# Attention with a gated convolution network on one core: neighbouring PSUM bank pairs, and exponentials that depend on all maxima of their score set

## The chip, the core and the metric

The kernel runs on one core of a Trainium2 chip. The core has five engines, each with its own in-order queue of instructions: TensorE (PE in the profile, with its weight loads shown as PEld), VectorE (DVE), ScalarE (ACT), GpSimd (POOL) and SyncE (SP, which issues DMAs). They meet through semaphores: an instruction can wait until another engine's semaphore has reached a value. Matmuls write into PSUM, which has eight banks of 512 float32 columns on 128 partitions; DVE and ACT read it. The metric is the device time of one execution in microseconds.

## What is computed

Eight batches, eight heads, 576 positions, head dimension 64. Attention is block causal with blocks of 64, and its output goes through a gated network with a convolution of width 3 along the sequence:

```python
scores = (1 / np.sqrt(D)) * np.matmul(q, k.transpose(0, 1, 3, 2))
scores = np.where(block_i >= block_j, scores, -1000000000.0)
scores = scores - np.max(scores, axis=-1, keepdims=True)
attn = np.exp(scores)
attn = attn / (np.sum(attn, axis=-1, keepdims=True) + 1e-09)
out = np.matmul(attn, v)
...
h = np.maximum(x @ w_in, 0.0)                      # x: heads side by side, 512 wide; h: 1024 wide
conv_out = sum(conv_w[k] * hp[:, k:k + S, :] for k in range(3))
gate = 1.0 / (1.0 + np.exp(-conv_out))
return h * gate @ w_out
```

The network's products are split into high and low parts (three products each), so FFN work takes the larger share of the matmul instructions' columns.

## The kernel before

**The work.** A visit handles two heads of one batch. The first batch is cut into a part A (blocks 0 to 3 of the sequence) and a part B (blocks 4 to 8); from the second batch on, a visit takes all nine blocks, and there are 28 such visits. The score matmuls (line L1000) of a visit come in sets that each fill two PSUM banks, one per head: blocks 8 and 5, blocks 7 and 6, and blocks 4, 3, 2, 1, 0 (in part A one set of four blocks, in part B the last set is block 4 alone). For each block of a set, DVE takes the row maxima of both heads in one instruction (`mx`, L1012, it reads both banks), and ACT one exponential for each head (`ex`, L1017, it reads one bank, writes the tile p and sums its rows). In the program an exponential depends on the maximum of its own block. A few small instructions on the statistics tile st then merge the two 32-row halves (L1031, L686, L1038 to L1052), POOL scales the probabilities (L1064), DVE transposes them (L1083), and PE multiplies them with v (L1096) into two more banks. From these ACT writes the high part of x (L1110), and DVE the low part (L1113); DVE reads both banks.

**The network (FFN).** When the four visits of a batch have written x, `ffn` multiplies with w_in (L1143, one bank per 128 columns of the hidden layer), ACT takes the relu (L1157) and one convolution tap (L1160), DVE the other two taps (L1164, L1168), ACT the tanh (L1173), DVE the gate (L1176), ACT and POOL make its high and low part (L1180, L1183), and PE multiplies with w_out (L1209) into one bank; ACT copies the result out (L1217) and SP stores it. FFN matmuls of one batch are mixed with the attention of the next. Dummy matmuls (L1304) fill planned gaps of PE.

**What sets the order.** All of this is recorded as operations with durations, dependencies and buffers. `Plan.order` then runs a list scheduler over them: each operation has a number in the table TARGETS (in twentieths of a microsecond) by which a ready operation is preferred, and the scheduler also hands out the PSUM banks. Its function `vacant` says whether banks are free for an operation that needs one or two; the loop at the end of `order` picks them. In the kernel before, the two banks of a set can be any two free ones: `both` makes a view of them with a step, so the pair (1, 4) is read as `banks[:, 1:5:3]`. The order that comes out is written engine by engine into the program, and the framework below derives the semaphore waits from what each instruction reads and writes.

Of the kernel before, what the change touches and what calls it, by code (L numbers as in the profile page):

```python
# [18 lines left out]
PE, DVE, ACT, POOL, SP = 0, 1, 2, 3, 4  # L19

TARGETS = """
# [238 lines left out]
class Plan:  # L260
# [53 lines left out]
    def order(self, targets, skip, fill, clock, pair):  # L314
# [26 lines left out]
        n = len(slots)  # L341
# [11 lines left out]
        def vacant(o, t):  # L353
# [3 lines left out]
            ask = {}  # L357
            for b in need:
                ask[b.tag] = max(ask.get(b.tag, 0), b.index + 1)
            at = sorted(freed[z] for z in range(n) if tenant[z] is None)  # L360
            if len(at) < len(need):
                return None, need
            own = kept[0] if t < kept[2] else kept[1]
# [30 lines left out]
        while left:  # L394
# [49 lines left out]
            t, _, e, o, where = best  # L444
# [896 lines left out]
```

## Time and profile before

| | |
|---|---|
| time, median of 3 runs | 851.78 us (849.61 to 852.69) |
| the profiled execution | 848.9 us, of which the span from first to last instruction is 847.0 us |
| PE busy | 722.5 us (85%) |
| DVE busy | 598.7 us (71%) |
| ACT busy | 536.1 us (63%) |
| POOL busy | 446.4 us (53%) |
| mean granted TensorE clock | 0.959 of full speed |
| chain of work that ended last, by engine | PE 20%, DVE 17%, ACT 16%, POOL 9% |

Busy times are unions of instruction spans, so an engine's idle time is the span less its busy time: 124.5 us on PE. In the lists of waits a line names the instruction before which an engine sat idle, and what ended the idle time; waits under 0.15 us are not counted. The granted clock is 1 at 2.4 GHz and 0.5 at 1.2 GHz.

### The profile page before, as it was taken

Reading aid. Unit: us, or ns where it says so; the run is one execution under the profiler, and the core shown is the slowest. Engines: PE = TensorE matmul, PEld = TensorE weight load, DVE = VectorE, ACT = ScalarE, POOL = GpSimd, SP = SyncE. Lnnn points to the kernel's source line nnn. Section 1 sums busy time; section 2 is a strip of 40 time slices with the busy share of each in tenths; the row PEclk is TensorE's granted clock in tenths of the full one; section 3 lists DMA queues with packets and bytes.
Section 4 is the critical chain, followed back from the end, with each engine's and each line's share of the span. In section 5 each row is a group of like instructions: output and inputs, shape, how many; then the busy total and the mean of one; then the engine's idle time right before and its main releaser. Section 6 shows DMA issues by size and latency. Waiting matters only on the chain.

```text
span 847.0 us, 29994 instructions
## 1 busy us (share of the span) xinstructions
PE 722.5 (85%) x12111; PEld 578.5 (68%) x12111; DVE 598.7 (71%) x1422; ACT 536.1 (63%) x1987; POOL 446.4 (53%) x926
## 2 busy tenths in 40 slices
PE   8788877777788898789989899879798968898998
PEld 6557656554666777476868677767676857677887
DVE  4698998665686858658777858677677836857453
ACT  5565656755676748457677658675677646567454
POOL 2455676554456553538456754556355725644332
PEclk9999999998999999899999999899999978999999
DMA  7925543334332422333313251333324232121001
GB/s 187 195 47 123 108 107 72 57 65 78 70 58 55 80 49 55 63 65 72 70 37 75 49 119 30 83 58 84 58 48 94 41 72 43 29 56 30 27 26 38
DMA packets 238671, 58.59 MB, mean 69 GB/s; under 512 B 228652, under 2 KB 233028, under 8 KB 238532
## 3 DMA queue, kind: packets, MB, share of 16 engines
q1 hardware_dynamic: 237988, 56.55, 32.0%
q8 instruction: 95, 1.56, 0.8%
q14 instruction: 44, 0.36, 0.2%
q10 hardware_dynamic: 544, 0.13, 0.1%
HBM read 47.21 MB, written 9.44 MB: 67 GB/s over the span
## 4 chain that ended last, share of the span: by engine, by line
PE 20%; DVE 17%; ACT 16%; POOL 9%; issue 4%; DMA 0%; POOLq 0%; SPq 0%; DVEq 0%; ACTq 0%
ACT p L1017 9%; PE banks L1143 9%; DVE st L1012 6%; POOL p L1064 6%; PE banks L1209 5%; PE banks L1000 3%; PE banks L1096 3%; DVE ptw L1083 3%; POOL gl L1183 2%; DVE t L1164 2%; ACT t L1160 2%; DVE t L1168 1%; ACT h L1157 1%; ACT t L1173 1%; DVE t L1176 1%
## 5 line engine op out<-in xcount | busy, mean ns | idle before, releaser
L1017 ACT ACTIVATE p<-banks,st 128x160 f32<-128x160 f32 (+8 forms) x576 | 221.3, 395 | 153.4 <-DVE st L1012 130.1
L1064 POOL TENSOR_SCALAR p<-p,st 128x32 f32<-128x32 f32 (+8 forms) x576 | 246.1, 445 | 120.2 <-DVE st L1052 110.5
L1143 PE MATMUL banks<-x,wih 128*128 128x290 f32 (+3 forms) x1024 | 206.7, 315 | 33.1 <-DVE st L1012 15.5
L1143 PEld LDWEIGHTS banks<-x,wih 128*128 128x128 f32 x1024 | 164.9, 199 | 54.2 <-DVE st L1012 18.1
L1012 DVE TENSOR_REDUCE st<-banks 128x2 f32<-128x320 f32 (+8 forms) x288 | 132.3, 481 | 90.8 <-ACT p L1017 34.2
L1183 POOL TENSOR_TENSOR gl<-t,gh 128x289 fp32r<-128x289 f32 (+3 forms) x128 | 109.5, 866 | 115.1 <-ACT gh L1180 102.9
L1083 DVE STREAM_TRANSPOSE ptw<-p 128x576 f32<-128x576 f32 (+8 forms) x272 | 130.4, 502 | 31.5 <-POOL p L1064 30.8
L1209 PE MATMUL banks<-woh,gh 128*128 128x512 f32 (+1 forms) x296 | 122.7, 414 | 24.1 <-DVE st L1012 14.8
L1000 PE MATMUL banks<-kT,qT 64*32 64x128 f32 (+8 forms) x4320 | 107.8, 316 | 22.7 <-DVE st L1012 5.0
L1143 PE MATMUL banks<-x,wil 128*128 128x288 f32 (+3 forms) x512 | 114.9, 311 | 11.3 <-DVE st L1012 7.1
L1209 PE MATMUL banks<-woh,gl 128*128 128x512 f32 (+1 forms) x296 | 118.4, 400 | 5.0 <-POOL gl L1183 4.7
L1017 ACT ACTIVATION_READ_ACCUMULATOR p<-banks,st 128x1 f32 x576 | 118.0, 205 | 0.0
L1209 PE MATMUL banks<-wol,gh 128*128 128x512 f32 (+1 forms) x296 | 116.9, 395 | 0.0
L686 POOL TENSOR_SCALAR st<-st 32x16 f32<-32x16 f32 (+2 forms) x136 | 32.8, 241 | 142.1 <-ACT p L1017 94.9
L1000 PEld LDWEIGHTS banks<-kT,qT 64*32 64x32 f32 x4320 | 70.1, 110 | 53.9 <-issue 15.3
L1164 DVE SCALAR_TENSOR_TENSOR t<-h,cw,t 128x289 f32<-128x289 f32 (+3 forms) x128 | 72.4, 573 | 42.3 <-ACT t L1160 40.4
L1096 PE MATMUL banks<-ptw,vn 64*32 64x224 f32 (+8 forms) x4608 | 93.9, 300 | 9.3 <-issue 6.1
L1143 PEld LDWEIGHTS banks<-x,wil 128*128 128x128 f32 x512 | 87.0, 200 | 17.1 <-DVE st L1012 9.8
L1096 PEld LDWEIGHTS banks<-ptw,vn 64*32 64x32 f32 x4608 | 80.6, 106 | 26.3 <-issue 10.7
L1209 PEld LDWEIGHTS banks<-woh,gh 128*128 128x128 f32 x296 | 57.0, 193 | 46.9 <-DVE st L1012 20.6
L1173 ACT ACTIVATE t<-t 128x289 f32<-128x289 f32 (+3 forms) x128 | 57.0, 447 | 33.0 <-DVE t L1168 32.1
L1157 ACT ACTIVATE h<-banks 128x290 f32<-128x290 f32 (+3 forms) x128 | 50.8, 407 | 40.5 <-PE banks L1143 30.9
(91 smaller groups left out, 859.1 us busy)
## 6 DMA issues: line engine op xcount, KB each, us to landing
vn<-in_v_dram SPq DMA_DIRECT2D x128, 144.0 KB, 3.7
out_dram<-stage SPq DMA_DIRECT2D x35, 256.0 KB, 2.1
qn<-in_q_dram SPq DMA_DIRECT2D x112, 72.0 KB, 2.8
kn<-in_k_dram SPq DMA_DIRECT2D x112, 72.0 KB, 2.6
x<-in_moe_w_out_dram SPq DMA_DIRECT2D x8, 512.0 KB, 4.1
gl<-in_moe_w_in_dram SPq DMA_DIRECT2D x4, 512.0 KB, 5.7
gh<-in_moe_w_in_dram SPq DMA_DIRECT2D x3, 512.0 KB, 4.1
vxa<-in_v_dram SPq DMA_DIRECT2D x16, 64.0 KB, 3.4
```

The costliest lines, as they stand in the source:

```text
L1000: nc.tensor.matmul(both(sb)[32 * quad:32 * quad + 32, h, o:o + w].rearrange("p (u n) -> p u n", n=32), t["q"].ap[r, 64 * b + 32 * g:64 * b ...
L1012: nc.vector.tensor_reduce(out=st.ap[:, c:c + 2], in_=both(sb)[:, :, off:off + w], op=ALU.max, axis=AX.X, negate=True)
L1017: nc.scalar.activation(out=pt.ap[:, h, :], in_=both(sb)[:, h, off:off + w], func=AF.Exp, bias=st.ap[:, c:c + 1], accum_out=st.ap[:, n + c: ...
L1064: nc.gpsimd.tensor_scalar(out=pt.ap[:, h, :], in0=pt.ap[:, h, :], scalar1=st.ap[:, 5 * n + c:5 * n + c + 1], scalar2=0.0, op0=ALU.mult, op ...
L1083: nc.vector.transpose(pt.ap[:, :, b:b + rise * b + 1:rise, :], x.ap.rearrange("p h (u n) -> p h u n", n=32))
L1096: nc.tensor.matmul(both(vb)[o:o + 32, g, 32 * (lo - b0):32 * (b1 - b0)].rearrange("p (b n) -> p b n", n=32), vat(u, h)[r, 32 * y:32 * y + ...
L1143: nc.tensor.matmul(fb.ap[:, 0:n2], wt[:, c, fs], xs[c][xi].ap[:, x0:x0 + n2], start=(n + c - c0 == 0), stop=(n + c - c0 == 3 * NCC - 1))
L1157: nc.scalar.activation(out=hb.ap[:, 0:n2], in_=fb.ap[:, 0:n2], func=AF.Relu, scale=0.5)
L1164: nc.vector.scalar_tensor_tensor(out=t.ap[:, i0:no], in0=hb.ap[:, own + i0 - 1:own + no - 1], scalar=cw[:, f:f + 1], in1=t.ap[:, i0:no], o ...
L1173: nc.scalar.activation(out=t.ap[:, 0:no], in_=t.ap[:, 0:no], func=AF.Tanh)
L1183: nc.gpsimd.tensor_tensor(out=gbuf[1].ap[:, f, carry:carry + no], in0=t.ap[:, 0:no], in1=gbuf[0].ap[:, f, carry:carry + no], op=ALU.subtract)
L1209: nc.tensor.matmul(fb.ap[:, 0:cut], gbuf[a].ap[:, f, cs], w[:, f, ds], start=(f == 0 and n == 0), stop=(f == NFC - 1 and n == 2))
```

## The change

Four edits, and a new table of numbers.

1. An operation that needs two banks gets an even bank and its right neighbour (0 and 1, 2 and 3, 4 and 5, 6 and 7); one that needs a single bank prefers one whose neighbour is taken. `both` is then a plain contiguous slice. This concerns the score sets (L1000, L1012, L1017) and the banks from which x is read (L1096, L1110, L1113).
2. In a score set all maxima are recorded before the exponentials, and each exponential depends on all of them.
3. The planner's durations for four small copies of the statistics (L1031, L686) are 0.23 and 0.26 in place of 0.15 and 0.2. They change no instruction.
4. TARGETS is another table of the same length. The count of every kind of instruction stays as it was, but for one dummy matmul more (173 for 172). The lines after the edits move by 10 to 13: L1000 is L1010, L1012 is L1023, L1017 is L1028, L1096 is L1109, L1113 is L1126, L1143 is L1156, L1209 is L1222.

```diff
--1214 -1250 -926 -958 -1097 -783 -1374 -1285 -1001 -1007 -709 -742 -948 -909 -960 -790 -625 -807 -914 -36 -288 91 883 731 552 -182 -412 857 -202 120
...
-            at = sorted(freed[z] for z in range(n) if tenant[z] is None)
-            if len(at) < len(need):
+            if len(need) == 2:
+                at = [max(freed[z], freed[z + 1]) for z in range(0, n, 2) if tenant[z] is None and tenant[z + 1] is None]
+            else:
+                at = [freed[z] for z in range(n) if tenant[z] is None]
+            if not at:
                 return None, need
...
-            return at[len(need) - 1], need
+            return min(at), need
...
+            need = [b for b in o.banks if b.slot is None]
+            if len(need) == 2:
+                z = min((max(freed[z] + o.ldw, freed[z + 1] + o.ldw, o.start), last[z] != need[0].tag, z)
+                        for z in range(0, n, 2) if tenant[z] is None and tenant[z + 1] is None)[2]
+                at = [z, z + 1]
+            elif need:
+                at = [min((max(freed[z] + o.ldw, o.start), tenant[z ^ 1] is None, last[z] != need[0].tag, z) for z in range(n) if tenant[z] is None)[3]]
+            for b, z in zip(need, at if need else ()):
+                last[z] = b.tag
...
         a, b = sorted(x.slot for x in pair)
-        return banks[:, a:b + 1:b - a]
+        assert b == a + 1
+        return banks[:, a:b + 1]
...
+            ms, todo = [], []
...
-                e = pl.op(DVE, c_dve(2 * w), mx, t0 + 0.6, deps=[o], bufs=sb + [st])
+                ms.append(pl.op(DVE, c_dve(2 * w), mx, t0 + 0.6, deps=[o], bufs=sb + [st]))
...
-                    es.append(pl.op(ACT, c_act(w, True, True, True) + 0.01, ex, t0 + 1.0 + 0.4 * h, deps=[e], bufs=sb + [st, pq[b]]))
+                    todo.append((w, ex, pq[b]))
+            for x, (w, ex, pt) in enumerate(todo):
+                es.append(pl.op(ACT, c_act(w, True, True, True) + 0.01, ex, t0 + 1.0 + 0.4 * x, deps=ms, bufs=sb + [st, pt]))
...
-            sw.append(pl.op(ACT if quad < 2 else POOL, 0.15 if quad < 2 else 0.2, swap, t0, deps=es, bufs=[st]))
+            sw.append(pl.op(ACT if quad < 2 else POOL, 0.23 if quad < 2 else 0.26, swap, t0, deps=es, bufs=[st]))
```

Two places show what this does to the order. The first is PE at the last visit of the second batch, where its score sets stand between matmuls with w_out. A name in brackets is the engine whose semaphore the instruction waits for. Before:

```order
L1000 MATMUL banks<-kT,qT 32x288 x8
L1000 MATMUL banks<-kT,qT 32x192 x8
L1209 MATMUL banks<-woh,gh 128x512 [waits DVE_49]
L1209 MATMUL banks<-wol,gh 128x512
L1209 MATMUL banks<-woh,gl 128x512
L1209 MATMUL banks<-woh,gh 128x512 [waits DVE_49]
L1209 MATMUL banks<-wol,gh 128x512
L1209 MATMUL banks<-woh,gl 128x512
L1000 MATMUL banks<-kT,qT 32x160 [waits DVE_49]
L1000 MATMUL banks<-kT,qT 32x160 x7
```

And at the same visit in the changed kernel, its sets (7, 6) and (4 to 0):

```order
L1222 MATMUL banks<-woh,gh 128x512 [waits Activation_49]
L1222 MATMUL banks<-wol,gh 128x512
L1222 MATMUL banks<-woh,gl 128x512 [waits Pool_49]
L1222 MATMUL banks<-woh,gh 128x512
L1222 MATMUL banks<-wol,gh 128x512
L1222 MATMUL banks<-woh,gl 128x512
L1010 MATMUL banks<-kT,qT 32x256 [waits DVE_49,Activation_49]
L1010 MATMUL banks<-kT,qT 32x256 x7
L1010 MATMUL banks<-kT,qT 32x224 x8
L1010 MATMUL banks<-kT,qT 32x160 [waits DVE_49]
L1010 MATMUL banks<-kT,qT 32x160 x7
```

The matmuls with w_out no longer wait for DVE; the score sets wait for DVE and ACT, whose instructions read those banks before.

The second place is DVE at the same visit: the maxima of its sets (7, 6) and (8, 5), which share the statistics tile st_2856, and those of blocks 4 to 0 (st_2936). Before:

```order
L1012 TENSOR_REDUCE st_2856<-banks 128x2 [waits PE_49]
L1012 TENSOR_REDUCE st_2856<-banks 128x2
L1012 TENSOR_REDUCE st_2856<-banks 128x2 [waits PE_49,Activation_49] x2
L1083 STREAM_TRANSPOSE ptw<-p_71 128x2x5x32 [waits Pool_49]
L1083 STREAM_TRANSPOSE ptw<-p_2773 128x2x3x32 [waits Pool_49]
L1083 STREAM_TRANSPOSE ptw<-p_2767 128x2x4x32 [waits Pool_49]
L1083 STREAM_TRANSPOSE ptw<-p_2752 128x2x2x32 [waits Pool_49]
L1083 STREAM_TRANSPOSE ptw<-p_2748 128x2x32 [waits Pool_49]
L1012 TENSOR_REDUCE st_2936<-banks 128x2 [waits PE_49,Activation_49]
L1012 TENSOR_REDUCE st_2936<-banks 128x2 [waits Activation_49]
L1012 TENSOR_REDUCE st_2936<-banks 128x2
L1012 TENSOR_REDUCE st_2936<-banks 128x2 [waits Activation_49]
```

After (the same blocks, st_2768 for the first two sets, st_2900 for blocks 4 to 0, st_2659 is of the visit ahead):

```order
L1023 TENSOR_REDUCE st_2768<-banks 128x2 [waits PE_49]
L1057 SCALAR_TENSOR_TENSOR st_2659<-st_2659 128x10 [waits Activation_49]
L1023 TENSOR_REDUCE st_2768<-banks 128x2
L1023 TENSOR_REDUCE st_2900<-banks 128x2 [waits PE_49]
L1023 TENSOR_REDUCE st_2900<-banks 128x2 x2
L1061 SCALAR_TENSOR_TENSOR st_2659<-st_2659 128x10 [waits DVE_49]
L1023 TENSOR_REDUCE st_2900<-banks 128x2
L1065 RECIPROCAL st_2659<-st_2659 128x10 [waits DVE_49]
L1023 TENSOR_REDUCE st_2900<-banks 128x2
```

The maxima of a set now wait once, for the score matmuls, and no longer for ACT's exponentials between them.

## Rows read from the trace of the kernel before

**Rows 1.** The head of the page and its first part: busy time of each engine, share of the span, instructions.

```profile
span 847.0 us, 29994 instructions
PE 722.5 (85%) x12111; PEld 578.5 (68%) x12111; DVE 598.7 (71%) x1422; ACT 536.1 (63%) x1987; POOL 446.4 (53%) x926
```

**Rows 2.** The view of the cores: span and mean granted TensorE clock.

```profile
core 0: 847.0 us, clock 0.959
```

**Rows 3.** The waits of PE: instruction that waited, what ended the wait, us in total, times, longest.

```profile
PE banks L1143 <- DVE st L1012: 22.6, 26, 2.2
PE banks L1209 <- DVE st L1012: 14.8, 15, 2.0
PE banks L1143 <- ACT h L1157: 7.8, 11, 2.7
...
PE banks L1000 <- DVE st L1012: 5.0, 6, 1.9
PE banks L1000 <- ACT p L1017: 5.0, 5, 3.4
...
PE banks L1000 <- DVE x L1113: 4.2, 2, 3.2
...
PE banks L1209 <- DVE x L1113: 3.3, 4, 0.9
...
PE banks L1209 <- ACT x L1110: 2.1, 3, 0.8
```

**Rows 4.** The waits of DVE before a maximum (same columns).

```profile
DVE st L1012 <- ACT p L1017: 34.2, 62, 1.8
...
DVE st L1012 <- PE banks L1000: 23.4, 17, 7.3
...
DVE st L1012 <- PE banks L1209: 9.8, 8, 2.3
...
DVE st L1012 <- PE banks L1143: 9.3, 14, 1.4
DVE st L1012 <- PE banks L1096: 9.1, 4, 3.1
...
DVE st L1012 <- PE banks L1304: 2.1, 2, 1.8
```

**Rows 5.** The waits of ACT for a maximum, before an exponential and before a relu (same columns).

```profile
ACT p L1017 <- DVE st L1012: 130.1, 118, 4.7
...
ACT h L1157 <- DVE st L1012: 7.0, 6, 2.8
```

**Rows 6.** The timeline at the place shown above (last visit of the second batch): start in us, duration, engine, line, operation; in brackets the idle time before it and what ended it.

```profile
188.76 1.16 DVE L1012 TENSOR_REDUCE st<-banks 128x2 f32<-128x448 f32 x2
...
189.98 0.51 PE L1209 MATMUL banks<-woh,gh 128*128 128x512 f32 x1 [0.89 <-DVE st L1012]
190.04 0.45 ACT L1017 ACTIVATE p<-banks,st 128x224 f32<-128x224 f32 x1 [1.85 <-DVE st L1012]
...
191.06 0.76 DVE L1012 TENSOR_REDUCE st<-banks 128x2 f32<-128x576 f32 x1 [1.13 <-ACT p L1017]
191.85 0.48 ACT L1017 ACTIVATE p<-banks,st 128x256 f32<-128x256 f32 x1 [0.84 <-DVE st L1012]
...
191.87 0.50 PE L1209 MATMUL banks<-woh,gh 128*128 128x512 f32 x1 [0.92 <-DVE st L1012]
...
192.94 0.56 DVE L1012 TENSOR_REDUCE st<-banks 128x2 f32<-128x384 f32 x1 [1.13 <-PE banks L1209]
...
193.54 0.47 ACT L1017 ACTIVATE p<-banks,st 128x256 f32<-128x256 f32 x1 [1.12 <-DVE st L1012]
...
193.56 0.70 PE L1000 MATMUL banks<-kT,qT 64*32 64x160 f32 x29 [0.72 <-DVE st L1012]
```

**Rows 7.** The timeline of PE at three longer stalls before FFN matmuls (columns as in rows 6).

```profile
149.08 0.56 PE L1143 MATMUL banks<-x,wil 128*128 128x322 f32 x2 [1.71 <-DVE st L1012]
...
347.15 0.50 PE L1209 MATMUL banks<-woh,gh 128*128 128x512 f32 x1 [1.96 <-DVE st L1012]
...
597.24 0.70 PE L1143 MATMUL banks<-x,wih 128*128 128x288 f32 x2 [2.15 <-DVE st L1012]
```

**Rows 8.** The view by stretches, right behind those three stalls: stretch, its length, busy time of each engine with its instructions, granted clock (PEclk), DMA share, GB/s.

```profile
150.30:153.70 3.40, 3.40 (x87) 2.91 (x86) 2.23 (x7) 3.35 (x14) 1.65 (x5) 0.50 0.00 0
...
348.30:355.10 6.80, 5.72 (x105) 2.85 (x110) 5.62 (x17) 4.20 (x20) 2.25 (x7) 0.50 0.44 95
...
597.50:600.80 3.30, 3.30 (x15) 3.30 (x15) 1.20 (x5) 2.69 (x16) 0.63 (x3) 0.50 0.97 172
```

**Rows 9.** The maxima by shape, from the groups of instructions: columns read (both heads together), count, busy us, mean ns of one, idle time before them and its releasers. A block b has 64 (b + 1) columns.

```profile
L1012 DVE TENSOR_REDUCE st<-banks 128x2 f32<-128x448 f32 x32 | 19.5, 610 | 8.1 <-PE banks L1096 3.1 <-ACT p L1017 1.2 <-PE banks L1000 1.1
...
L1012 DVE TENSOR_REDUCE st<-banks 128x2 f32<-128x384 f32 x32 | 17.4, 542 | 6.7 <-ACT p L1017 2.0 <-PE banks L1304 1.8 <-PE banks L1209 1.7
...
L1012 DVE TENSOR_REDUCE st<-banks 128x2 f32<-128x256 f32 x32 | 13.2, 414 | 9.4 <-ACT p L1017 5.0 <-PE banks L1209 2.8 <-PE banks L1000 0.8
...
L1012 DVE TENSOR_REDUCE st<-banks 128x2 f32<-128x192 f32 x32 | 11.2, 351 | 8.9 <-ACT p L1017 6.0 <-PE banks L1143 1.6 <-PE banks L1209 1.3
...
L1012 DVE TENSOR_REDUCE st<-banks 128x2 f32<-128x128 f32 x32 | 9.1, 283 | 10.5 <-ACT p L1017 4.5 <-PE banks L1143 2.6 <-PE banks L1096 2.3
...
L1012 DVE TENSOR_REDUCE st<-banks 128x2 f32<-128x64 f32 x32 | 7.0, 218 | 16.6 <-PE banks L1000 9.7 <-ACT p L1017 6.2 <-PE banks L1143 0.5
```

More of the change, by code (lines that the diff above doesn't have):

```diff
@@ L488, in order @@
                 o.lat = moved + 0.4 - o.end
-            for b in o.banks:
-                if b.slot is None:
-                    z = min((max(freed[z] + o.ldw, o.start), last[z] != b.tag, z) for z in range(n) if tenant[z] is None)[2]
-                    last[z] = b.tag
-                    b.slot, tenant[z] = z, b
-                    o.after += past[z]
-                    taken[b.tag] = max(taken[b.tag], b.index + 1)
+            need = [b for b in o.banks if b.slot is None]
[7 more added lines that the diff above has]
+                last[z] = b.tag
+                b.slot, tenant[z] = z, b
+                o.after += past[z]
+                taken[b.tag] = max(taken[b.tag], b.index + 1)
+            for b in o.banks:
                 b.left -= 1
```

361 rows, old and new, of the table TARGETS are left out of this document.

## The prediction

> **What bounds the kernel now.** I read the page's first part, then the waits of PE, DVE and ACT, then the timeline at one place, then the granted clock behind some stalls. PE is busy 722.5 of 847.0 us, so it idles 124.5 us [rows 1]; no other engine is busy over 71%. Filling PE's gaps is what can shorten the kernel, so the question is what ends them. The list of PE's waits has a surprise at its top: FFN matmuls, which need x and the weights, sit idle until a row maximum on DVE ends, 22.6 us before L1143 and 14.8 us before L1209 [rows 3], together 37.4 us or 30% of all idle time of PE. Neither matmul uses a maximum. The timeline shows how it happens [rows 6]: at 189.98 a matmul with w_out starts after 0.89 us of idling, when two maxima end; at 191.87 the next one again, when the maximum of block 8 ends; that maximum had waited 1.13 us for an exponential of the other set, and the maximum of block 5 at 192.94 waits 1.13 us for the w_out matmul. PE, DVE and ACT take turns where they could run beside each other.
>
> The two built programs say why. For each wait I looked up the instruction that raises the semaphore to the awaited value and compared the banks of both. In this visit the first set lies in banks 1 and 4 and the second in 0 and 6, while the w_out matmuls write bank 3. A view with a step from bank 1 to bank 4 is taken for everything between, bank 3 too. In the whole program 56 waits of FFN matmuls (34 at L1143, 22 at L1209) name a maximum, and in 50 of them the two share no bank; the same holds for 46 of 46 waits of a maximum for L1143, L1209, L1096 or L1304. In the changed program no wait of PE for a maximum, and none of a maximum for PE, is without a common bank; FFN matmuls name a maximum 7 times. Waits of a maximum for an exponential fall from 101 to 4, those of an exponential for a maximum from 164 to 82. So the change does what it says, and no instruction is removed; waits and order are all that changes.
>
> **Term 1, FFN matmuls and maxima.** 37.4 us of PE idling [rows 3] times 50/56 for the false share: 33.4 us that go. Bounds: nothing, if another wait of the same matmul ends just as late, and 37.4.
>
> **Term 2, w_out matmuls and x.** L1209 sits idle 3.3 us for the low part of x and 2.1 us for the high part [rows 3]. It reads neither; in the program all 8 of these waits are without a common bank before, and after the change the 2 that are left share one. 5.4 us go. L1143 does read x, so its waits for x stay.
>
> **Term 3, the clock.** Behind three of the stalls of term 1, of 1.71, 1.96 and 2.15 us [rows 7], the granted clock is 0.50 for 3.4, 6.8 and 3.3 us [rows 8], which is the lower of its two levels, 1.2 GHz; PE is busy in nearly all of that time. At 2.4 GHz the same work would take about half: (3.4 + 6.8 + 3.3) / 2 = 6.8 us. Over the run the mean clock is 0.959 [rows 2], so about 8% of the span, 69 us, is spent at the lower level, and 35 us is the most that a full clock could give back. I take 6.8, with ends 0 and 35.
>
> **Term 4, maxima first.** The exponential of a set's first block now starts after the last maximum of the set. Held back by the other maxima that is 0.542 us for set (8, 5), 0.610 us for (7, 6), 0.414 + 0.351 + 0.283 + 0.218 = 1.266 us for blocks 4 to 0, and 0.852 us for a set of part A [rows 9]; with 32, 32, 28 and 4 of them 17.3 + 19.5 + 35.4 + 3.4 = 75.7 us in all. But before, the maxima were not free to run beside the exponentials: DVE idles 34.2 us at maxima for exponentials, and 30.3 us (9.8 + 9.3 + 9.1 + 2.1) at maxima for matmuls of other banks [rows 4], and ACT idles 130.1 us in 118 pieces at exponentials for maxima [rows 5]. The turns of rows 6 show it: exponential, maximum, exponential, each after the end of the one before. Putting the maxima first changes the order inside a chain that was serial, so I cost it at nothing. What covers it are the other transposes, convolution taps and copies that the planner puts on DVE and ACT meanwhile; without this cover it costs up to 75.7 us, and the other end is the 64.5 us of DVE idling that go.
>
> The Trainium skill, PSUM — Partial Sum Buffer, section PSUM bank collisions raise a hardware error, says that two engines on the same bank and partitions at once are an error, reads against reads included. By that rule maximum and exponential of one set could never overlap, and term 4 is nothing; where they could overlap, it would be up to 75.7. The 1.13 us before the maximum at 191.06 agree that they take turns, though there the banks were different ones, and no run here shows such a collision.
>
> **Term 5, pairs.** A set now needs two adjacent free banks, held until its last exponential. Bank waits that are real become more: waits of score and v matmuls for an exponential go from 61 to 84 in the program, and waits of score matmuls for the low part of x from 4 to 14. Before, these cost 5.0 us (L1000 for p) and 4.2 us (L1000 for x) [rows 3]. Scaled with the counts that is 5.0 x 23/61 = 1.9 us and 4.2 x 10/4 = 10.5 us more: 12.4 us come back. Bounds: 0, if other work covers them, and twice that.
>
> **Term 6, the rest of the order.** The new table moves nearly every row on every engine. At the two ends of PE's queue, where least can run beside, little changes: behind the last v matmul stand 174 matmuls of L1143's kind in place of 168 and 144 of L1209's as before, and 6 more cost at most 6 x 0.28 = 1.7 us (two take 0.56 us in rows 7); the first FFN matmul stands behind 160 score and 94 dummy matmuls in place of 208 and 128, which can only help. SP's loads are the same DMAs in another order. I take 0, with ends of 1.7 us more and, for the 34 dummies, 17 us less (34 dummies at most 0.50 us each, the length of a matmul of the same 512 columns in rows 6).
>
> **Sum.** -33.4 - 5.4 - 6.8 + 0 + 12.4 + 0 = -33.2 us. The profiled execution took 848.9 us (span 847.0), 2.9 below the median of the three runs, 851.78. Against the execution the forecast is 815.7, against the median 818.6; I say 819.
>
> **Rivals.**
>
> *The stalls only move.* PE reaches its next wait sooner and waits there: for relu outputs, x, or score banks. For it: of 124.5 us of idling 87 us have other enders than these maxima. Against it: those waits are spread, 7.8 us for a group (L1143 for a relu that frees its bank) and less [rows 3]. If a quarter of terms 1 to 3 survives, 11 us, and term 5 shows little, the gain is about 10 us: 842.
>
> *The attention chain shortens as well.* DVE gets back 64.5 us of idling [rows 4], and half of ACT's 130.1 us at exponentials [rows 5] if waits go with their count, 164 to 82. x, the gates and the score banks then come earlier too, and PE's other idle time, 124.5 - 37.4 - 5.4 = 81.7 us, falls by a quarter, 20 us: 819 - 20 = 799. For it: relus behind those exponentials wait 7.0 us for maxima [rows 5], which is pure queueing. Against it: the work of DVE and ACT is the same in sum, and each chain keeps its steps.
>
> *Slower: exponentials held back.* Each first exponential waits for the whole set, its banks stay taken, and the next score matmul, for which PE stops, waits with them. Place: L1010 of the changed program before the sets of blocks 4 to 0, where the delay is 1.266 us. The price is the exposed share of 75.7 us, against 45.6 us from terms 1 to 3: it decides from a share of 60% on. At four fifths it is 75.7 x 0.8 - 45.6 = +15 us: 867. For it: waits of matmuls on exponentials rise by count. Against it: rows 6, where the exponentials come late anyhow.
>
> The Trainium skill, PSUM — Partial Sum Buffer, section Engine vs sequencer instructions, calls ScalarE's queue strictly first in, first out, which speaks for this rival: relus and copies behind a held exponential wait too. The 7.0 us of rows 5 agree; by that rule alone the delay on ACT could be the whole 75.7 us, where by rows 6 it is near nothing.
>
> **How the numbers follow.** About 0.5%, 4.3 us, is what a measurement of this kernel can tell from no change. Forecast, a gain of 18 to 46 us (806 to 834): 0.53. Stalls move, a gain of 0 to 18: 0.21, of which 0.07 within 0.5%. Attention shortens too, a gain above 46: 0.17. Slower: 0.09. So faster 0.53 + 0.14 + 0.17 = 0.84, same 0.07, slower 0.09. The range leaves out the slower case, most of the unchanged one and the last 0.04 below: 798 to 847.
>
> **What would show it.** Right: PE's waits for maxima before L1156 and L1222 under 6 us together; no idling of a maximum until an exponential; ACT's idling for maxima near half; PE's idle time near 90 us; the clock above 0.959. Term 5 is too low if L1010 waits for p, st or x by over 25 us together, and term 4 is wrong if ACT's idling at exponentials for maxima stays near 130 us. The prediction falls if PE's idle time stays above 115 us with the false waits gone: then they were cover for something else.

## The result and the profile after

The changed kernel takes 748.51 us (median of 4 runs, 746.76 to 750.95), the kernel before 851.48 us beside it: a ratio of 0.8794, interval 0.8764 to 0.8824. The gain is 103 us. The forecast was 819 us, a gain of 33, and the time lies below its range. The profiled execution took 750.95 us, 2.4 above the median of its kernel; that of the kernel before took 848.9, 2.6 below, so the spans below differ by 5 us less than the medians.

The head of the page and its first part, which answer to [rows 1]:

```profile
span 749.2 us, 29948 instructions
PE 687.9 (92%) x12112; PEld 562.6 (75%) x12112; DVE 588.6 (79%) x1422; ACT 528.2 (71%) x1987; POOL 447.2 (60%) x926
```

The view of the cores, as [rows 2]:

```profile
core 0: 749.2 us, clock 0.993
```

The span is 97.8 us shorter (847.0 less 749.2). PE's idle time went from 124.5 to 61.3 us (749.2 less 687.9), which is 63.2 of it. The other 34.6 us are PE's own busy time, 722.5 to 687.9, with the same matmuls and one dummy more. The granted clock goes with it. Its mean gives the time at the lower level: 2 x (1 - 0.959) x 847.0 = 69.5 us before, 2 x (1 - 0.993) x 749.2 = 10.5 us after. Half of the difference, 29.5 us, is most of the 34.6; the other 5 us were not traced.

The longest waits of PE (as [rows 3]: instruction, what ended the wait, us in total, times, longest), the two of score and FFN matmuls for x, and the one of score matmuls for a relu:

```profile
PE banks L1109 <- issue: 9.9, 13, 3.2
PE banks L1010 <- ACT p L1028: 7.7, 10, 1.4
PE banks L1222 <- POOL gl L1196: 7.2, 9, 1.5
...
PE banks L1156 <- DVE x L1126: 1.7, 1, 1.7
PE banks L1156 <- ACT h L1170: 1.6, 3, 1.0
...
PE banks L1010 <- DVE x L1126: 1.5, 2, 0.9
...
PE banks L1010 <- ACT h L1170: 0.8, 1, 0.8
PE banks L1010 <- ACT x L1123: 0.8, 1, 0.8
...
PE banks L1222 <- DVE x L1126: 0.5, 1, 0.5
```

The two waits that led [rows 3], FFN matmuls for a maximum with 37.4 us, are gone. Score matmuls (L1010) wait 10.0 us for p and x together (7.7 + 1.5 + 0.8). Waits that are not among the false ones of the prediction fell too: L1156 for a relu from 7.8 to 1.6 us.

The waits of DVE before a maximum (as [rows 4]), and of ACT for one (as [rows 5]):

```profile
DVE st L1023 <- PE banks L1010: 5.6, 11, 1.2
```

```profile
ACT p L1028 <- DVE st L1023: 42.2, 38, 4.9
```

No maximum idles for an exponential any more (34.2 us before), and ACT's idling at exponentials for maxima fell from 130.1 to 42.2 us, further than the number of such waits in the program (164 to 82). The timeline at one place, to be read beside [rows 6]:

```profile
170.41 0.67 DVE L1023 TENSOR_REDUCE st<-banks 128x2 f32<-128x512 f32 x1
...
170.86 1.08 ACT L1230 ACTIVATE stage<-banks 128x512 f32<-128x512 f32 x2
...
170.92 0.50 PE L1222 MATMUL banks<-woh,gh 128*128 128x512 f32 x1
...
171.08 1.08 DVE L1023 TENSOR_REDUCE st<-banks 128x2 f32<-128x448 f32 x3
171.25 0.40 PE L1222 MATMUL banks<-wol,gh 128*128 128x512 f32 x1
...
171.82 0.49 ACT L1028 ACTIVATE p<-banks,st 128x256 f32<-128x256 f32 x1
```

Here w_out matmuls and maxima run side by side, three more maxima follow the first without a wait, and the exponential of the first block starts 0.74 us after the end of its maximum (170.41 + 0.67 = 171.08), while ACT copies outputs. No bracket stands behind any of these rows: none of the three engines idled before them.

### The profile page after: what moved, and what is told of

Read it like the earlier page. It is cut to its first block, busy times and chain, and to the rows that moved or that the text cites. A ratio compares the mean times of both kernels' runs of the same rounds, so it can differ in the third digit from the quotient of the medians.

```text
span 749.2 us, 29948 instructions
## 1 busy us (share of the span) xinstructions
PE 687.9 (92%) x12112; PEld 562.6 (75%) x12112; DVE 588.6 (79%) x1422; ACT 528.2 (71%) x1987; POOL 447.2 (60%) x926
## 4 chain that ended last, share of the span: by engine, by line
DVE 34%; ACT 18%; PE 17%; POOL 13%; issue 7%; DMA 5%; SPq 4%; DVEq 0%; POOLq 0%; ACTq 0%
ACT p L1028 11%; POOL p L1077 10%; DVE st L1023 7%; DVE ptw L1096 6%; PE banks L1222 6%; PE banks L1156 5%; DVE t L1177 4%; PE banks L1109 4%; DVE t L1181 4%; DVE t L1189 3%; PE banks L1010 2%; POOL gl L1196 2%; DMA kn<-in_k_dram 2%; ACT t L1173 2%; SPq L721 2%
## 5 line engine op out<-in xcount | busy, mean ns | idle before, releaser
L1077 POOL TENSOR_SCALAR p<-p,st 128x160 f32<-128x160 f32 (+8 forms) x576 | 247.7, 448 | 84.4 <-DVE st L1065 80.8
L1028 ACT ACTIVATE p<-banks,st 128x32 f32<-128x32 f32 (+8 forms) x576 | 220.4, 401 | 61.8 <-DVE st L1023 42.2
L1156 PE MATMUL banks<-x,wih 128*128 128x290 f32 (+3 forms) x1024 | 191.1, 302 | 4.2 <-DVE x L1126 1.7
L1156 PEld LDWEIGHTS banks<-x,wih 128*128 128x128 f32 x1024 | 156.1, 189 | 17.8 <-issue 4.2
L1096 DVE STREAM_TRANSPOSE ptw<-p 128x448 f32<-128x448 f32 (+8 forms) x272 | 131.6, 504 | 38.7 <-POOL p L1077 34.9
L1023 DVE TENSOR_REDUCE st<-banks 128x2 f32<-128x192 f32 (+8 forms) x288 | 127.3, 471 | 6.3 <-PE banks L1010 5.6
L1222 PE MATMUL banks<-woh,gl 128*128 128x512 f32 (+1 forms) x296 | 117.9, 398 | 7.7 <-POOL gl L1196 7.2
L1028 ACT ACTIVATION_READ_ACCUMULATOR p<-banks,st 128x1 f32 x576 | 122.8, 213 | 0.0
L1222 PE MATMUL banks<-woh,gh 128*128 128x512 f32 (+1 forms) x296 | 119.6, 404 | 1.1 <-ACT h L1170 0.6
L1222 PE MATMUL banks<-wol,gh 128*128 128x512 f32 (+1 forms) x296 | 115.7, 391 | 0.8 <-POOL wol L846 0.8
L1109 PE MATMUL banks<-ptw,vn 64*32 64x160 f32 (+8 forms) x4608 | 94.9, 300 | 22.1 <-issue 9.7
L1010 PE MATMUL banks<-kT,qT 64*32 64x96 f32 (+8 forms) x4320 | 100.7, 303 | 14.3 <-ACT p L1028 7.7
L1109 PEld LDWEIGHTS banks<-ptw,vn 64*32 64x32 f32 x4608 | 82.1, 107 | 39.9 <-issue 13.9
L1156 PE MATMUL banks<-x,wil 128*128 128x290 f32 (+3 forms) x512 | 108.8, 299 | 0.0
L1010 PEld LDWEIGHTS banks<-kT,qT 64*32 64x32 f32 x4320 | 66.7, 105 | 43.0 <-ACT p L1028 14.2
L1156 PEld LDWEIGHTS banks<-x,wil 128*128 128x128 f32 x512 | 82.8, 190 | 2.1 <-issue 1.3
L1186 ACT ACTIVATE t<-t 128x287 f32<-128x287 f32 (+3 forms) x128 | 56.4, 446 | 30.8 <-DVE t L1181 30.0
L1222 PEld LDWEIGHTS banks<-woh,gl 128*128 128x128 f32 x296 | 55.8, 189 | 28.7 <-POOL gl L1196 17.0
L1181 DVE SCALAR_TENSOR_TENSOR t<-h,cw,t 128x288 f32<-128x288 f32 (+3 forms) x128 | 73.0, 579 | 1.0
L1189 DVE SCALAR_TENSOR_TENSOR t<-t,h 128x287 f32<-128x287 f32 (+3 forms) x128 | 64.7, 511 | 10.0 <-ACT t L1186 9.6
```

The source lines that it names most:

```text
L1010: nc.tensor.matmul(both(sb)[32 * quad:32 * quad + 32, h, o:o + w].rearrange("p (u n) -> p u n", n=32), t["q"].ap[r, 64 * b + 32 * g:64 * b ...
L1023: nc.vector.tensor_reduce(out=st.ap[:, c:c + 2], in_=both(sb)[:, :, off:off + w], op=ALU.max, axis=AX.X, negate=True)
L1028: nc.scalar.activation(out=pt.ap[:, h, :], in_=both(sb)[:, h, off:off + w], func=AF.Exp, bias=st.ap[:, c:c + 1], accum_out=st.ap[:, n + c: ...
L1077: nc.gpsimd.tensor_scalar(out=pt.ap[:, h, :], in0=pt.ap[:, h, :], scalar1=st.ap[:, 5 * n + c:5 * n + c + 1], scalar2=0.0, op0=ALU.mult, op ...
L1096: nc.vector.transpose(pt.ap[:, :, b:b + rise * b + 1:rise, :], x.ap.rearrange("p h (u n) -> p h u n", n=32))
L1109: nc.tensor.matmul(both(vb)[o:o + 32, g, 32 * (lo - b0):32 * (b1 - b0)].rearrange("p (b n) -> p b n", n=32), vat(u, h)[r, 32 * y:32 * y + ...
```

## The experiments

Names: a run whose name begins with a_ is the changed kernel with one edit, b_ the kernel before with one edit. The kernel before was timed beside each, and the ratio is against it. Line numbers of the maximum, the exponential, the score, w_in and w_out matmuls shift by a few from kernel to kernel. A false wait is one between two instructions that share no bank. Two theories stood at the start: A, the gain comes from the false waits that are gone; B, it comes from the new order, with the maxima first. Later runs name the theories that they tell apart.

### The false waits alone

**a_perm2 and a_perm4: the banks renumbered.** The pairs of the changed kernel are laid two, or four, banks apart, and nothing else is changed; every queue keeps its order.

```diff
-    psum = [banks[:, z] for z in range(8)]
+    PERM = (0, 2, 1, 3, 4, 6, 5, 7)
+    psum = [banks[:, PERM[z]] for z in range(8)]
...
-        return banks[:, a:b + 1]
+        a, b = PERM[a], PERM[b]
+        return banks[:, a:b + 1:b - a]
```

In a_perm4 PERM is (0, 4, 1, 5, 2, 6, 3, 7).

> The changed kernel with its order, its table and its rules as they are; only the places of the eight PSUM banks are exchanged, so that each pair lies two banks apart (0 and 2, 1 and 3, 4 and 6, 5 and 7) and the view of a pair has a step again and covers one bank of others. Built, 57 waits of FFN matmuls for a maximum are without a common bank, 250 such waits in all (before: 50 and 210, after: 0 and 3). Theory A, the false waits carry the gain, stalls and clock together: most of the 103 us are lost again, 815 to 850, PE idle over 105 us, clock 0.97 or less. Theory B, the new order carries it and the waits only moved with it: under 770.

> As the run before, but each pair lies four banks apart (0 and 4, 1 and 5, 2 and 6, 3 and 7), so that a view covers three banks of others: 104 waits of FFN matmuls for a maximum are false, 491 in all. Theory A: clearly slower than with step two, 860 to 920, clock 0.95 or less. Theory B: under 780.

Measured: 820.94 us (ratio 0.9653, 0.9585 to 0.9721) and 956.32 us (1.1227, 1.1156 to 1.1298). PE's longest waits with pairs four apart:

```profile
PE banks L1158 <- DVE st L1025: 38.7, 49, 2.0
PE banks L1224 <- DVE st L1025: 32.3, 31, 3.4
```

The waits that [rows 3] show are back, with nothing but the numbers of the banks changed. With pairs two apart, 57 waits of FFN matmuls are false (50 in the kernel before) and 72 us are lost (820.94 less 748.51), about the 66 us that b_split (below) gains by their removal in the old order. With pairs four apart, 104 are false, and the new order is slower than the kernel before. The first run is as theory A expected, but for a clock of 0.974 where it said 0.97 or less; the second lies above the expected range. DVE is busy 588.0 and 586.2 us (588.6 in the changed kernel), so it is not that the stepped views themselves are read more slowly: the false waits cost the time.

**b_split: the other way round.** The kernel before with its table and its order of work, in which an instruction that read two banks in one stepped view is cut into two that read one bank each (324 more on DVE, 36 on ACT). The same cut is made at the exponential's view and at both parts of x.

```diff
-                    nc.vector.tensor_reduce(out=st.ap[:, c:c + 2], in_=both(sb)[:, :, off:off + w], op=ALU.max, axis=AX.X, negate=True)
+                    one_, two_ = sorted(x.slot for x in sb)
+                    for h, z in enumerate((one_, two_)):
+                        nc.vector.tensor_reduce(out=st.ap[:, c + h:c + h + 1], in_=banks[:, z, off:off + w], op=ALU.max, axis=AX.X, negate=True)
```

> The kernel before, its table and order unchanged, but every instruction that read two banks through a stepped view is cut into two that read one bank each: 288 maxima and 36 low parts more on DVE, 36 high parts more on ACT. No false wait of an FFN matmul for a maximum is left (3 false in all); maxima wait for exponentials as before (106 waits). DVE has some 25 to 45 us more work. Theory A: 785 to 815, clock 0.975 or more, though the order was not made for it. Theory B: 835 or more, since the order is old and DVE has more to do.

Measured: 785.27 us (0.922, 0.9169 to 0.9272), at the lower end. PE's longest waits:

```profile
PE banks L1147 <- ACT h L1161: 10.1, 11, 2.7
PE banks L1000 <- ACT p L1019: 9.3, 15, 1.7
```

The view of the cores:

```profile
core 0: 782.7 us, clock 0.987
```

No FFN matmul waits for a maximum, with no pairs and no new order. PE's idle time falls by 41.8 us (124.5 to 82.7), close to the 38.8 of terms 1 and 2, its busy time by 22.5 (722.5 to 700.0). Some 37 us to the changed kernel are left.

**a_anytwo: edit 1 undone, planned again.** The scheduler hands out any two banks again, with the changed kernel's other edits and table (the added and removed lines are those of the diff of the change, reversed). The planner then puts in 231 dummy matmuls where it had 173, so this run is not as clean as the two above.

> The changed kernel with only the first edit undone: a set takes any two free banks, as before, with the new table and the exponentials depending on all maxima. 81 false waits of FFN matmuls for a maximum, 280 in all. Theory A: 830 to 870, no better than before, for the second edit and the new table gain little without pairs. Theory B: 760 to 790.

Measured: 871.92 us (1.0235, 1.018 to 1.0291), just above what was expected. PE waits for maxima before w_in and w_out matmuls:

```profile
PE banks L1146 <- DVE st L1013: 26.9, 39, 1.9
PE banks L1212 <- DVE st L1013: 23.5, 24, 2.0
```

### What the other 37 us are

**a_split: old order against new, without false waits in either.** The changed kernel with reads cut as in b_split.

```diff
-                    nc.vector.tensor_reduce(out=st.ap[:, c:c + 2], in_=both(sb)[:, :, off:off + w], op=ALU.max, axis=AX.X, negate=True)
+                    for h, z in enumerate(sorted(x.slot for x in sb)):
+                        nc.vector.tensor_reduce(out=st.ap[:, c + h:c + h + 1], in_=banks[:, z, off:off + w], op=ALU.max, axis=AX.X, negate=True)
```

> The changed kernel in its own order, but with each read of two banks cut into two reads of one bank (324 more instructions on DVE, 36 more on ACT), as in the kernel before with cut reads (785.27 us), so that the two differ by order alone. Theory E (the 37 us between 785.27 and 748.5 are mostly the price of the cut reads): 775 to 795 us. Theory O (they are the new order, with maxima first in it): 748 to 763 us, as the cut reads are covered by other work.

Measured: 757.57 us (0.8864, 0.8817 to 0.8911). Theory E falls. With the ratios times 851.48 us the gain splits like this: 66.4 us for the false waits (1 to 0.922), 30.3 us for the new order with edit 2 (0.922 to 0.8864), 6.0 us for the reads that need not be cut (0.8864 to 0.8794). Each ratio is uncertain by about 0.005 or 4 us, so the last step is barely told from nothing. In the spans, the step from b_split to a_split is 27.3 us (782.7 less 755.4): 18.5 of PE's idle time and 8.8 of its busy time (700.0 to 691.2).

**b_split_late and b_late: edit 2 put into the old order.** Each exponential that stands ahead of its set's last maximum is moved right behind it; only ACT's queue changes.

```diff
+    for ms, xs_ in sets:
+        y = max(at[id(o)] for o in ms)
+        for o in xs_:
+            if at[id(o)] < y:
+                key[id(o)] = (y, 1, at[id(o)])
+    for o in sorted(plan, key=lambda o: key[id(o)]):
+        o.fn()
```

> The kernel before with cut reads (785.27 us) and edit 2 alone put into its order: each exponential that stood ahead of the last maximum of its set is moved to just behind it. PE, DVE, POOL and SP keep their order; on ACT 220 of 1451 places change. Waits of a maximum for an exponential fall from 106 to 8. Theory M (maxima first is worth time by itself, as DVE no longer waits for ACT inside a set): 760 to 777 us. Theory O (it is worth something only where the whole order was searched with it): 780 to 792 us. The rival of held-back exponentials: over 795 us.

> The kernel before with the same move of exponentials behind the last maximum of their set, and with its false waits kept (57 of FFN matmuls for a maximum, 50 of them without a common bank). On ACT 211 of 1415 places change, on the other engines none. Theory M: 825 to 845 us (a gain of 7 to 25, with the false waits still there). Theory O: 847 to 857 us. Held-back exponentials: over 860 us, since a maximum that waits for a matmul now holds the whole set.

Measured: 819.35 us (0.9591, 0.9547 to 0.9635), 34 us more than b_split, and 875.55 us (1.0242, 1.0188 to 1.0297), 22 us more than the kernel before beside it (853.81). Maxima first makes the old order slower, with the false waits and without them. The waits show the trade. DVE's idling at maxima for exponentials falls, in b_split and then in b_split_late:

```profile
DVE st L1014 <- ACT p L1019: 19.1, 47, 1.3
```

```profile
DVE st L1017 <- ACT p L1023: 1.3, 1, 1.3
```

Score matmuls wait 18.2 us for exponentials in place of 9.3:

```profile
PE banks L1003 <- ACT p L1023: 18.2, 17, 3.9
...
L1003 PE MATMUL banks<-kT,qT 64*32 64x288 f32 x480 | 26.7, 440 | 19.6 <-ACT p L1023 14.0 <-ACT stage L1226 2.6 <-DVE st L1055 1.4
```

That is the mechanism of the prediction's slower rival, but not its place: it named the sets of blocks 4 to 0, and 14.0 of the 18.2 us stand before block 8 (the score matmuls of 288 columns), in the set (8, 5).

**b_split_flip and a_flip: the waits alone.** Here no queue changes at all. Every engine gets the same instructions in the same order, from the same banks; only the direction of the wait between an exponential and a maximum of its set is turned, wherever that closes no ring of waits. In a_flip the next maximum waits for the exponential, as before the change:

```diff
+                prev = ms_[y - 1]
+                x = ms.index(prev)
+                for e in xs_[2 * x:2 * x + 2]:
+                    u, v = at[id(e)], at[id(m_)]
+                    if not reach(v, u):
+                        outs[u].add(v)
```

In b_split_flip the exponentials wait for all maxima, as after the change:

```diff
+            for m_ in ms:
+                for e in xs_:
+                    u, v = at[id(m_)], at[id(e)]
+                    if not reach(v, u):
+                        outs[u].add(v)
```

> The changed kernel with every engine's queue instruction for instruction as it is (PE, DVE, ACT, POOL and SP differ at no place) and with the same banks, but with the waits of edit 2 turned round wherever that makes no ring: the exponential of a block no longer waits for the next maximum of its set, the next maximum waits for the exponential. Waits of a maximum for an exponential rise from 4 to 53. In the kernel before 101 of them came with 34.2 us of idling on DVE, 0.34 us each, so 49 more make 17 us. Theory M (maxima first is worth time by itself): 754 to 770 us. Theory O (the order carries the gain, the waits inside a set are covered): 745 to 753 us. Held-back exponentials cost time: under 745 us.

> The mirror of the run a_flip: the kernel before with cut reads (785.27 us), every queue instruction for instruction as it is, with the waits inside a set turned to maxima first wherever that makes no ring. Waits of a maximum for an exponential fall from 106 to 8; exponentials wait for the last maximum of their set. Theory M (a maximum that waits for ACT is a loss in any order): 755 to 778 us, a gain near the 33 us that a_flip lost. Theory W (what counts is that waits and order are planned together: waits turned against the order cost time in either direction): 790 to 825 us. Waits inside a set covered in this order: 780 to 790 us.

Measured: a_flip 782.0 us (0.9154, 0.9107 to 0.92), 33 us more than the changed kernel; b_split_flip 846.88 us (0.9962, 0.9936 to 0.9988), 62 us more than b_split. Both lie above every range that was expected of them. In a_flip the maxima idle where they did not:

```profile
DVE st L1025 <- ACT p L1030: 47.7, 44, 3.4
```

Each of these waits is 1.08 us long (47.7 / 44), twice the 0.55 us of [rows 4] (34.2 / 62), and 44 of 53 waits in the program show up as idling, where it was 62 of 101; so the expected 17 us were too few. In b_split_flip ACT stands before exponentials, in b_split it did so for 84.2 us:

```profile
ACT p L1023 <- DVE st L1017: 156.8, 75, 13.4
```

```profile
ACT p L1019 <- DVE st L1014: 84.2, 88, 3.5
```

What is queued behind them comes late to PE, in b_split_flip:

```profile
PE banks L1152 <- ACT h L1166: 15.8, 11, 4.8
PE banks L1152 <- ACT stage L1226: 8.9, 5, 4.1
```

In b_split w_in matmuls waited 10.1 us for a relu and 2.2 for an output copy. The Trainium skill, PSUM — Partial Sum Buffer, section Engine vs sequencer instructions, states that ScalarE's queue is strictly first in, first out. These rows agree: relus (h) and output copies (stage) need no maximum, and pay for one.

So neither theory M nor theory O alone holds. Turning the rule round costs 33 us in the order that was searched with it, and bringing it into the order that was not costs 22 to 62 us (b_late, b_split_late, b_split_flip). With its waits turned the new order takes 782.0 us, about the 785.27 of b_split: in these runs neither the rule nor the order gained anything by itself. A turned wait also meets queues that were laid out for the other direction, so the 33 us are the price of rule and order at odds, and no run gives the worth of edit 2 alone in an order made without it.

**a_early: edit 2 undone in the new order, with ACT's queue changed.** Each exponential is moved ahead to just behind its own maximum, or as near as its buffer allows (795 of ACT's 1415 places change).

```diff
+        for x, o in enumerate(xs_):
+            y = max([at[id(d)] for d in o.deps if d not in ms] + [at[id(ms[x // 2])]])
+            if y < at[id(o)]:
+                key[id(o)] = (y, 1, x)
```

> The changed kernel with edit 2 alone undone in its order: each exponential is moved ahead to just behind the maximum of its own block, or as near to it as its buffer allows. PE, DVE, POOL and SP keep their order and the banks stay; waits of a maximum for an exponential rise from 4 to 141. Theory M: 765 to 785 us. Theory O: 745 to 757 us. If exponentials held back cost anything in the changed kernel, it comes out below 746 us.

Measured: 891.33 us (1.0442, 1.0396 to 1.0488), far above all expectations and 109 us above a_flip. Moving exponentials ahead pushes relus, taps and gates back on ACT, and w_in matmuls wait for relus:

```profile
PE banks L1160 <- ACT h L1174: 27.1, 19, 6.0
```

This run changes order and waits at once, so it bears on the value of the order more than on edit 2.

**a_free: pairs or not.** The changed kernel with cut reads and unchanged queues, with the banks dealt anew, the one that comes free first.

```diff
+                    z = min((max(freed[z] + o.ldw, o.start), last[z] != b.tag, freed[z], z) for z in range(8) if tenant[z] is None)[3]
+                    place[id(b)], rest[id(b)], tenant[z], last[z] = z, len(b.uses), b, b.tag
+                    b.slot = z
```

> The changed kernel with cut reads (757.57 us) and every queue as it is, but with its banks dealt anew and no longer in pairs: each operation takes the bank that comes free first. Term 5 of the prediction (pairs cost 12.4 us, since score and v matmuls wait for neighbours): 742 to 750 us. Theory that pairs cost nothing in this order: 752 to 763 us.

Measured: 757.33 us (0.8883, 0.8821 to 0.8946) against 757.57 for a_split. No cost of the pairs shows in this order, within the 5 us that the runs can tell: score matmuls wait 8.4 us for exponentials here and 9.6 in a_split.

### Idle time and the clock over the runs

Each row is one profiled execution; the time at the lower level is 2 x (1 - mean clock) x span.

| kernel | span us | PE idle us | mean clock | us at 1.2 GHz |
|---|---|---|---|---|
| after | 749.2 | 61.3 | 0.993 | 10 |
| a_split | 755.4 | 64.2 | 0.991 | 14 |
| a_free | 754.8 | 67.4 | 0.995 | 8 |
| a_flip | 779.4 | 83.3 | 0.980 | 31 |
| b_split | 782.7 | 82.7 | 0.987 | 20 |
| b_split_late | 814.6 | 105.3 | 0.973 | 44 |
| a_perm2 | 817.2 | 110.5 | 0.974 | 42 |
| a_anytwo | 871.8 | 124.1 | 0.954 | 80 |
| before | 847.0 | 124.5 | 0.959 | 69 |
| b_split_flip | 847.1 | 128.0 | 0.948 | 88 |
| b_late | 875.9 | 142.1 | 0.947 | 93 |
| a_early | 891.7 | 151.2 | 0.931 | 123 |
| a_perm4 | 952.1 | 191.0 | 0.921 | 150 |

Where PE idles clearly more, it also spends more time at the lower level: against the changed kernel, 0.5 to 1.3 us more for each us of idling more (a_split and a_free aside, which differ too little, and a_anytwo, which has 58 dummies more). Neighbours in the list can be the other way round: a_free idles 6 us more than the changed kernel and spends less time at the lower level. PE's busy time, of the same matmuls, grows by 0.4 to 0.6 us for each us of idling more (8.2 us for 22.0 in a_flip, 73.2 for 129.7 in a_perm4). This is a relation over the runs; no run changed the stalls alone and nothing else.

## Why the prediction was wrong, step by step

**What bounds the kernel, and the false waits: right.** They are the largest part of the gain (a_perm2, a_perm4 and b_split). What was to show it came: waits of PE for maxima before L1156 and L1222 at nothing, no idling of a maximum until an exponential, the clock above 0.959. Two other signs were too timid: PE's idle time, said to be near 90 us (the terms of the sum make it 98), came to 61.3, and ACT's idling for maxima, said to be near half, to a third (42.2 of 130.1). What failed is the sum, at term 3, at term 5, and at terms 4 and 6 together.

**Terms 1 and 2, 38.8 us: right, a little low.** The waits that they are taken from sum to 42.8 us and fell to 0.5 (L1222 for the low part of x). In b_split, where the order is the old one, PE's idle time falls by 41.8.

**Term 3, 6.8 us: the step that failed first.** It counted three stretches of 13.5 us at the lower level, because those had been looked at, while the same paragraph put 69 us of the span there. 59 of the 69 us went (69.5 to 10.5). Half of that is 29.5 us, inside the stated end of 35 and four times the value taken. The Trainium skill, TensorE: Matmul & The Clock Gate, section HAM oscillation — how this bites in real kernels, prices time at the lower clock at half its length. The fall of PE's busy time by 34.6 us agrees to 5 us. In b_split the clock gives back (69.5 - 20.3) / 2 = 24.6 us, and PE's busy time falls by 22.5.

**Term 5, 12.4 us to come back: did not come.** It scaled idle time by the number of waits in the program. The counts did rise as given (61 to 84 and 4 to 14), and the idle time of score matmuls for p, st and x fell, from 14.2 us (5.0 + 5.0 + 4.2) to 10.0. The part for p rose from 5.0 to 7.7, near the 6.9 that the term gives; the part for x, where the term has 14.7, fell from 4.2 to 2.3. Taking the pairs away again gains nothing (a_free, where p costs 8.4 us). The number of semaphore waits says how many instructions could be held up, not how long.

**Terms 4 and 6, each costed at nothing: 30.3 us together**, of which the clock's share (8.8 us of PE's busy time) is part of term 3's shortfall too. Term 4 asked what edit 2 does to the order before, and term 6 asked what the new table does, each by itself. By itself edit 2 cost 22 to 62 us in the old order, inside term 4's bound of 75.7; in the new one, turning it round costs 33. The two can't be priced apart, and the sum had no term for the two together.

**The rivals.** "The attention chain shortens as well" came closest: PE's other idle time, 81.7 us, was to fall by a quarter, 20 us, and it fell by 20.9, to 60.8 (61.3 less the 0.5). That the number fits is luck, for no row gave the quarter, and the cause that it names does not suffice. It expected the fall from the idle time that DVE and ACT get back. In b_split they get a part of it back (maxima idle 19.1 us for exponentials instead of 34.2, exponentials 84.2 us for maxima instead of 130.1), and PE's other idle time stays, at 82.7 us. In b_split_late maxima idle only 1.3 us for exponentials, and PE idles 105.3. It is with the new order that PE's idle time falls (64.2 in a_split, with the same cut reads). Its 799 us came out too high because it kept term 3 and the 12.4 us of term 5. "Exponentials held back" is a real mechanism too, seen in b_split_late, b_late and b_split_flip, in an order that was not made for it. "The stalls only move" holds for a small part: idling before v matmuls rose from 11.2 to 24.0 us, and that of w_out matmuls for gl from 4.7 to 7.2; all other idling of PE fell by far more, from 108.6 to 30.1 us.

In the spans, the forecast's error is 97.8 - 33.2 = 64.6 us: 27.8 in PE's busy time (34.6 against 6.8), 33.3 in its other idle time (a fall of 20.9 against a rise of 12.4), and 3.5 in terms 1 and 2.

What stays open: which places of the new order the 30 us come from, and whether an order searched without edit 2 and without false waits would come as low. Edit 3 was not tried alone.

## What to carry to other kernels

Where an engine waits for something that it does not need, look at what the two instructions touch in common: a view with a step over banks is taken for all that lies between, and the waits can be got rid of by adjacent banks or by reads of one bank each. When stalls of PE are to go, look at the clock for all of the time at the lower level, not only behind the stalls that you looked at. A rule of waiting and the order that was made for it must be judged together: here turning it round cost 33 us in one order, and bringing it in cost 22 to 62 in the other.

## What was not expected of the hardware

The time at the lower clock grows with the stalls over the whole range of the runs, from 10 us at 1.2 GHz with 61 us of PE idling to 150 us with 191, so that in a_perm4 PE is busy 761.1 us with the matmuls that take 687.9 us in the changed kernel. And 324 more instructions on DVE (605.8 us busy in a_split, 588.6 in the changed kernel) cost 6 to 9 us, with an uncertainty of 4 or more, about half of the 17 us that they add to DVE's busy time, though DVE is busy in about 80% of the span.
